# Two rows of x stored early into the output by ScalarE, in a one-core decode layer

## The chip, the cores and the metric

The kernel runs on one core of a Trainium2 chip. The metric is device time in microseconds (us), from one launch; lower is better. Three runs of the kernel before gave 137.84, 137.99 and 138.12 us, median 137.99.

A core has TensorE (PE in the profile; its weight loads are PEld), VectorE (DVE), ScalarE (ACT), GpSimd (POOL) and SyncE (SP). SP and ACT issue transfers; each has a queue of its own, and the packets of both run on the same 16 DMA engines.

## The reference

One decoding step (one token for each of 4 sequences) of a pre-norm layer: attention over the last 2048 cached keys with 32 query heads on 4 key-value heads, then a gated feed-forward. Cut to what is computed:

```
h  = x + A(layernorm(x))
h2 = h + B(layernorm(h))                      # the output, 4 x 1 x 1024, bf16

A(x):  q = x @ wq                             # wq 1024 x 4096
       p = softmax(q k^T * Dh**-0.5)          # k, v: the last 2048 of 8192 rows, 4 batches, 4 kv heads
       return (p v) @ wo                      # wo 4096 x 1024
B(x):  return (silu(x @ w1) * (x @ w3)) @ w2  # w1, w3 1024 x 3584, w2 3584 x 1024
```

All inputs are bf16. Nearly all bytes are weights and cache; x itself is 8 KB.

## The kernel before, in words

The kernel is a single stream of loads with work hung on it. `plan` lists the loads in order: wq (with a narrow "side" load that brings the end of its last rows in 1 KB pieces), the keys, the values, wo, w1, w3 and w2 in four pieces of 17, 7, 3 and 1 rows. `load_next` issues the next entry, always from SP (L94, L102, L120, L126), into a ring of 80K columns in SBUF. A piece is issued as soon as its place in the ring is free, which is when TensorE has read what lay there.

The stages follow the loads: the first norm and q (L178 to L282), the transposes of k and the scores (L312 to L332), softmax (L335 to L361), the values (L379 to L389), wo (L409 to L417), the second norm (L423 to L451), the gate w1 and the up projection w3 (`gate_up`, L454), and the down projection w2 (`down`, L490). The wide tiles hold four column blocks one below the other: partition 32j + 8b of a wide tile holds column block j of sequence b. `x_q` is x in that form, 256 columns for each j and b, the other partitions zero. It is loaded by two DMAs of SP (L169) and read only once, where it is added to the attention's output (L424).

Around the change: the gate's product `g_ps` goes through ScalarE's exponential into `eg` (L471, with a table load before it), VectorE makes `1/(1 + eg)` and multiplies it with the gate (L472 to L475), TensorE does w3, VectorE multiplies and transposes (L478, L481), TensorE does w2. The two halves of the result are copied into `res` by VectorE (L513) and ScalarE (L514), and ScalarE issues the one store of the output (L515): 16 rows of `res`, 512 bytes each. ScalarE computes nothing between L471 and L514.

The tile framework orders the work. Each DMA gets one of eight completion semaphores ("lanes" 0 to 7, `DMAHW0` to `DMAHW7`) in turn. A DMA that takes a lane waits until the lane's previous DMA has landed; a reader waits for the lane of the DMA that it needs. An instruction holds few waits, so further ones stand ahead of it on the same engine as instructions that only wait. At the end of the program (L541) SP goes through all lanes and the engines' semaphores in five waits, two semaphores each, in this order: lanes 3 and 2, lanes 4 and 1, lanes 5 and 0, lane 6 and VectorE, lane 7 and ScalarE. Then the engines meet at two barriers and the program ends. In the kernel before, the four pieces of w2 have lanes 3, 4, 5 and 6, and the output's store has lane 7.

Of the kernel before, what the change touches and what calls it, by code (L numbers as in the profile page):

```python
# [11 lines left out]
ACT = mybir.ActivationFunctionType  # L12
# [7 lines left out]
def kernel(  # L20
# [13 lines left out]
    nc = tc.nc  # L34
# [15 lines left out]
    out_flat = out.flatten_outer_dims()  # L50
# [16 lines left out]
    RS = QD // B  # L67
    CQ = Hq * Dh // JG
    CG = D // JG
    CF = F // JG  # L70
    HF = CF // 2
# [94 lines left out]
    x_q = act.tile([P, CG], BF16)  # L166
    nc.vector.memset(x_q[:], 0.0)
    for c in range(2):
        nc.sync.dma_start(  # L169
            out=x_q[c * 2 * QD : (c + 1) * 2 * QD : RS, :],  # L170
            in_=x_flat.rearrange("b (j c) -> j b c", j=JG)[2 * c : 2 * c + 2],
# [7 lines left out]
    for c in range(2):  # L179
# [8 lines left out]
        out=xn[:], in0=x_sb[:], scalar1=mv[:, 0:1], scalar2=rstd[:, 0:1],  # L188
# [14 lines left out]
    for r0, ne, ns in SETS:  # L203
# [3 lines left out]
            out=xs[:, len(sl) : len(sl) + ns, : ne * 4].rearrange("b l (i s) -> b l i s", s=4),  # L207
            in_=v[:, KC - 1, :, :, :],
        )
        for l in range(ns):  # L210
            nc.tensor.transpose(
                out=ts_ps[: ne * 4, len(sl), :], in_=xs[:, len(sl), : ne * 4], identity=ident[:B, :B]
# [4 lines left out]
    for _, ne, ns in SETS:  # L217
# [14 lines left out]
        out=perm[:].rearrange("p (h dq) -> p h dq", dq=JG),  # L232
        in_=ident[:].rearrange("p (dq h) -> p h dq", dq=JG),
# [12 lines left out]
    for j in range(2, JG):  # L246
        nc.vector.tensor_tensor(
            out=same[:, 0, :], in0=same[:, 0, :], in1=ident[:, j * QD : (j + 1) * QD], op=ALU.add
# [35 lines left out]
    for r in range(REP):  # L284
        nc.tensor.transpose(out=qt_ps[:, r, :], in_=q_sb[:, r * Dh : (r + 1) * Dh], identity=ident[:])
    nc.vector.tensor_copy(
        out=qz[:, :, : Hkv * QD].rearrange("p b (g z) -> p b g z", g=Hkv)[:, :, :, :REP],
        in_=qt_ps[:].rearrange("p r (g x) -> p x g r", g=Hkv)[:, :B, :, :],
# [24 lines left out]
    for u, (b, n) in enumerate(units):  # L313
        k_v = loaded["k"][b]
        kT = ktpool.tile([P, NJ, P], BF16, tag="kT")
        for t in range(NJ // TB):
            kt_ps = psA.tile([P, TB, P], BF16, tag=f"kt{nt % 4}")
            for jj in range(TB):
                nc.tensor.transpose(  # L319
                    out=kt_ps[:, jj, :], in_=k_v[:, n * NJ + t * TB + jj, :], identity=ident[:]  # L320
# [21 lines left out]
        out=Pm[:], in_=scores_ps[:], func=ACT.Exp, bias=nmax[:], scale=1.0, accum_out=rsum[:]  # L342
# [6 lines left out]
    for c in range(NSB):  # L349
# [4 lines left out]
        for g in range(Hkv):  # L354
            if g % 2 == 0:
                nc.vector.tensor_scalar(  # L356
                    out=z[:, :, g, :], in0=pt_ps[:], scalar1=mask[:, g : g + 1], scalar2=None, op0=ALU.mult
# [10 lines left out]
        out=Dm[:], in0=ident[:].rearrange("p (g b r) -> p b g r", g=Hkv, b=B),  # L368
# [38 lines left out]
    g_ps = psB.tile([P, 2, 512], FP32, tag="g")  # L407
    u_ps = psB.tile([P, 2, 512], FP32, tag="u")
    for i in range(IO):  # L409
# [34 lines left out]
        out=hn[:], in0=h1[:], scalar1=tot[:, 0:1], scalar2=rstd2[:, 0:1],  # L444
# [5 lines left out]
        out=hnT[:].rearrange("p k x -> p (k x)"), in_=hn[:].rearrange("q (c k) -> q k c", k=KC)  # L450
# [3 lines left out]
    def gate_up(kind, out_ps):  # L454
# [13 lines left out]

    gate_up("w1", g_ps)
    eg = wide.tile([P, 2, HF], FP32, tag="w4k")  # L470
    nc.scalar.activation(out=eg[:], in_=g_ps[:, :, :HF], func=ACT.Exp, scale=-1.0)  # L471
    nc.vector.tensor_scalar_add(out=eg[:], in0=eg[:], scalar1=1.0)  # L472
    nc.vector.reciprocal(out=eg[:], in_=eg[:])  # L473
    gs = wide.tile([P, 2, HF], FP32, tag="w4k")
# [7 lines left out]
        out=hgT[:].rearrange("p i x -> p (i x)"),  # L482
        in_=hg[:].rearrange("q s c -> q (s c)").rearrange("q (c i) -> q i c", i=IF),
# [62 lines left out]
```

## Time and profile before

| what | value |
|---|---|
| three runs, median (lowest to highest) | 137.99 us (137.84 to 138.12) |
| span of the profiled execution | 136.0 us |
| HBM read | 55.59 MB, 409 GB/s over the span |
| packets of SP's queue (q1), share of 16 engines | 95.6% |
| packets of ScalarE's queue (q10) | 36, 0.02 MB |
| busy: PE, PEld, DVE, ACT, POOL | 72.3, 46.1, 43.9, 31.0, 1.7 us |

The span runs from the first to the last instruction. The profile gives the profiled execution no time of its own beyond its span; the median of the runs is 1.99 us above it, and that difference is taken as what lies around the span. A share of 95.6% of all 16 DMA engines says that the loads hardly ever pause. Line numbers are those of the kernel before; from L472 on, the same statement stands two lines further down after the change.

### The profile page before, as it was taken

To read this page: it belongs to the slowest core of one execution; us is meant where nothing else is said; L and a number is where in the kernel's file an instruction comes from. 1 tells how busy PE (TensorE), PEld (TensorE's weight loads), DVE (VectorE), ACT (ScalarE), POOL (GpSimd) and SP (SyncE) were. 2 spreads that over 40 slices of the span, in tenths; PEclk is the share of its full clock that TensorE was granted. 3 is DMA by queue.
4 is the path that set the end of the run, shared out by engine and by line. 5 is a ranking of instruction groups with operands and counts; after the bars stand their busy time and mean duration, and the time that the engine had idled before them with its cause. 6 is when DMAs were issued, how large, how long until landed. Compare 5 with 4: busy or idle time off the path is not lost.

```text
span 136.0 us, 2436 instructions
## 1 busy us (share of the span) xinstructions
PE 72.3 (53%) x1096; PEld 46.1 (34%) x1096; DVE 43.9 (32%) x79; ACT 31.0 (23%) x36; POOL 1.7 (1%) x8
## 2 busy tenths in 40 slices
PE   0004920979898989810525916791097000970981
PEld 0002300268374756500014905570043000430870
DVE  5055000043344444470994001206200596026010
ACT  3000000015555555609294300000001400000000
POOL 5000000000000000000000000000000000000000
PEclk9999975557999999985555555568556855568568
DMA  5999999999999999999989999989989899999970
GB/s 155 464 463 406 412 420 414 429 424 439 424 439 424 424 443 426 410 552 453 463 347 463 463 410 405 477 354 494 439 371 494 371 472 401 399 420 407 424 298 5
DMA packets 2650, 55.75 MB, mean 410 GB/s; under 512 B 296, under 2 KB 464, under 8 KB 720
## 3 DMA queue, kind: packets, MB, share of 16 engines
q1 hardware_dynamic: 2604, 55.58, 95.6%
q8 instruction: 8, 0.13, 0.3%
q10 hardware_dynamic: 36, 0.02, 0.0%
q14 instruction: 2, 0.02, 0.0%
HBM read 55.59 MB, written 0.01 MB: 409 GB/s over the span
## 4 chain that ended last, share of the span: by engine, by line
DMA 54%; PE 25%; ACT 11%; DVE 5%; SPq 2%; issue 1%; ACTq 0%
DMA ring<-in_B_w_dram 38%; DMA ring<-in_A_wq_dram 15%; PE kt_ps L319 11%; ACT kT L325 5%; PE scores_ps L304 5%; ACT z L360 3%; PE q_ps L263 3%; DVE rmax L336 2%; ACT Pm L341 2%; PE OT_ps L382 2%; DVE pT L350 1%; SPq L120 1%; PE g_ps L459 1%; DVE z L356 1%; ACT L341 1%
## 5 line engine op out<-in xcount | busy, mean ns | idle before, releaser
L325 ACT COPY kT<-kt_ps 128x1024 bf16<-128x1024 bf16 x16 | 15.9, 1013 | 13.4 <-PE kt_ps L319 13.4
L319 PE MATMUL kt_ps<-ident,ring 128*128 128x128 bf16 x256 | 18.0, 232 | 0.0
L319 PEld LDWEIGHTS <-ring 128*128 128x128 bf16 x256 | 16.0, 105 | 4.9 <-issue 4.9
L323 DVE COPY kT<-kt_ps 128x1024 bf16<-128x1024 bf16 x16 | 11.1, 692 | 16.5 <-PE kt_ps L319 16.5
L459 PEld LDWEIGHTS <-hnT 128*32 128x32 bf16 x128 | 5.5, 143 | 21.8 <-issue 19.2
L382 PE MATMUL OT_ps<-z,ring 128*128 128x32 bf16 x256 | 7.5, 188 | 8.5 <-ACT z L360 5.0
L459 PE MATMUL u_ps<-ring,hnT 128*32 128x448 bf16 x64 | 6.0, 563 | 11.0 <-DMA ring<-in_B_w_dram 11.0
L304 PE MATMUL scores_ps<-kT,qz 128*32 128x512 bf16 x64 | 9.9, 609 | 2.9 <-ACT kT L325 2.9
L263 PE MATMUL q_ps<-ring,xnT 128*4 128x512 bf16 x63 | 6.7, 595 | 7.8 <-DMA ring<-in_A_wq_dram 7.8
L382 PEld LDWEIGHTS <-ring 128*128 128x128 bf16 x256 | 7.4, 104 | 9.2 <-issue 9.2
L459 PE MATMUL g_ps<-ring,hnT 128*32 128x448 bf16 x64 | 5.9, 558 | 4.9 <-DMA ring<-in_B_w_dram 4.9
L492 PEld LDWEIGHTS <-hgT 128*32 128x32 bf16 x156 | 4.9, 134 | 6.2 <-issue 5.7
L411 PE MATMUL y_ps<-ring,o 128*32 128x256 bf16 x128 | 5.9, 371 | 0.8 <-DVE o L398 0.8
L514 ACT CAST res<-yb_ps 128x128 bf16<-128x128 f32 x1 | 0.3, 266 | 26.1 <-PE yb_ps L492 26.1
L492 PE MATMUL y_ps<-ring,hgT 128*32 128x256 bf16 x68 | 3.8, 419 | 4.4 <-DMA ring<-in_B_w_dram 4.4
L360 ACT ACTIVATE z<-pt_ps,mask 128x512 bf16<-128x512 f32 x8 | 5.3, 687 | 3.5 <-DVE z L356 3.5
L352 PE MATMUL pt_ps<-pT,perm 128*128 128x512 bf16 x4 | 2.4, 607 | 6.8 <-DVE pT L350 6.8
L263 PEld LDWEIGHTS <-xnT 128*4 128x4 bf16 x63 | 2.0, 115 | 11.7 <-issue 11.6
L194 PE MATMUL tp_ps<-ident,xn 4*128 4x4 bf16 x8 | 0.7, 200 | 10.0 <-DVE xn L187 10.0
L356 DVE TENSOR_SCALAR z<-pt_ps,mask 128x512 bf16<-128x512 f32 x8 | 5.5, 741 | 1.2 <-ACT z L360 0.8
L473 DVE RECIPROCAL eg<-eg 128x896 f32<-128x896 f32 x1 | 5.8, 5753 | 0.0
L411 PEld LDWEIGHTS <-o 128*32 128x32 bf16 x128 | 4.4, 131 | 3.1 <-DVE o L398 1.9
(85 smaller groups left out, 50.1 us busy)
## 6 DMA issues: line engine op xcount, KB each, us to landing
ring<-in_B_w_dram SPq DMA_DIRECT2D x2, 7168.0 KB, 22.5
ring<-in_A_k_cache_dram SPq DMA_DIRECT2D x4, 2048.0 KB, 27.6
ring<-in_A_v_cache_dram SPq DMA_DIRECT2D x4, 2048.0 KB, 29.2
ring<-in_B_w_dram SPq DMA_DIRECT2D x1, 4352.0 KB
ring<-in_A_wq_dram SPq DMA_DIRECT2D x1, 4096.0 KB, 12.2
ring<-in_A_wq_dram SPq DMA_DIRECT2D x1, 3968.0 KB
ring<-in_B_w_dram SPq DMA_DIRECT2D x1, 1792.0 KB
ring<-in_B_w_dram SPq DMA_DIRECT2D x1, 768.0 KB
```

The lines of the kernel that those rows point to most:

```text
L263: nc.tensor.matmul(q_ps[QD * g : QD * g + B, hf * 512 : hf * 512 + n], lhsT=xnT[:, kc, :], rhs=wq_t[:, c0 : c0 + n], start=(kc == 0), stop ...
L304: nc.tensor.matmul(scores_ps[QD * g : QD * (g + 1), n * 512 : (n + 1) * 512], lhsT=qz_v[:, z0 : z0 + QD], rhs=kT_v[:, g, :, :], start=(b = ...
L319: nc.tensor.transpose(out=kt_ps[:, jj, :], in_=k_v[:, n * NJ + t * TB + jj, :], identity=ident[:])
L323: nc.vector.tensor_copy(out=kT[:, t * TB : (t + 1) * TB, :], in_=kt_ps[:])
L325: nc.scalar.copy(out=kT[:, t * TB : (t + 1) * TB, :], in_=kt_ps[:])
L356: nc.vector.tensor_scalar(out=z[:, :, g, :], in0=pt_ps[:], scalar1=mask[:, g : g + 1], scalar2=None, op0=ALU.mult)
L360: nc.scalar.mul(out=z[:, :, g, :], in_=pt_ps[:], mul=mask[:, g : g + 1])
L382: nc.tensor.matmul(OT_ps[:, b, :], lhsT=loaded["v"][b][:, j, :], rhs=PTz[j // NJ][:, (j % NJ) * B + b, :, :], start=(j == 0), stop=(j == J ...
L411: nc.tensor.matmul(y_ps[QD * j : QD * (j + 1), :], lhsT=o4[:, i, :, :].rearrange("p b s -> p (b s)"), rhs=loaded["wo"][i][:, j * CG : (j + ...
L459: nc.tensor.matmul(out_ps[QD * j : QD * (j + 1), hf, :HF], lhsT=hnT[:, k, :], rhs=loaded[kind][k][:, c0 : c0 + HF], start=(k == 0), stop=( ...
L473: nc.vector.reciprocal(out=eg[:], in_=eg[:])
L492: nc.tensor.matmul(out_ps[QD * j : QD * (j + 1), :n], lhsT=hgT[:, i, :], rhs=loaded["w2"][i][:, j * CG + c0 : j * CG + c0 + n], **kw,)
```

## The change

Behind the exponential, ScalarE also issues a store of two rows of `x_q` (partitions 0 and 8: the first 256 columns of x for sequences 0 and 1) into the first 256 columns of the output's rows 0 and 1, 512 bytes each. `tc.issue_after` places it behind the exponential in ScalarE's order. The output's store at the end writes these places again, so that the output is the same.

```diff
     gate_up("w1", g_ps)
     eg = wide.tile([P, 2, HF], FP32, tag="w4k")
-    nc.scalar.activation(out=eg[:], in_=g_ps[:, :, :HF], func=ACT.Exp, scale=-1.0)
+    exp_i = nc.scalar.activation(out=eg[:], in_=g_ps[:, :, :HF], func=ACT.Exp, scale=-1.0)
+    with tc.issue_after(exp_i.ins):
+        nc.scalar.dma_start(out=out_flat[0:2, 0:CG], in_=x_q[0 : 2 * RS : RS, :])
     nc.vector.tensor_scalar_add(out=eg[:], in0=eg[:], scalar1=1.0)
```

In the built program two more things differ. The early store takes lane 3, so every DMA behind it moves on by one lane: the pieces of w2 have lanes 4 to 7, the output's store lane 0. And the output's store, which writes where the early store wrote, waits for lane 3 (the early store) beside its own lane, VectorE and ScalarE:

```
before  L515 DMACopy out_dram<-res 4x4x256 [waits DMAHW7_49,DVE_49,Activation_49]
after   L473 DMACopy out_dram<-x_q 2x256 [waits DMAHW4_49,DMAHW3_49]
after   L517 DMACopy out_dram<-res 4x4x256 [waits DMAHW0_49,DMAHW3_49,DVE_49,Activation_49]
```

The order of all other instructions on every engine is the same, and so is the order of SP's five waits at the end.

## The prediction

> **What bounds the kernel now.** I read the page's queue table first, then the chain that ended last, then the timeline and the transfers of the last microseconds.
>
> ```profile
> span 136.0 us, 2436 instructions
> ...
> q1 hardware_dynamic: 2604, 55.58, 95.6%
> ...
> q10 hardware_dynamic: 36, 0.02, 0.0%
> ...
> DMA 54%; PE 25%; ACT 11%; DVE 5%; SPq 2%; issue 1%; ACTq 0%
> ```
>
> SP's queue q1 keeps the 16 DMA engines busy for 95.6% of the span: the stream of weights is the bound. In the chain, in order of time, the end reads:
>
> ```profile
> 76.27 22.49 DMA ring<-in_B_w_dram
> ...
> 98.80 1.68 PE g_ps L459 x14
> 100.48 29.74 DMA ring<-in_B_w_dram
> ...
> 130.27 0.30 PE ya_ps L492 x3
> ```
>
> From 76 us to 130.2 us the chain is nothing but weights landing, save 1.7 us. So whatever delays the stream delays the end, and whatever lies on ScalarE or VectorE between 100 and 130 us does not, unless it is long. The timeline of that stretch and of the end:
>
> ```profile
> 106.06 0.92 ACT L471 ACTIVATE eg<-g_ps 128x896 f32<-128x896 f32 x1
> ...
> 107.67 5.75 DVE L473 RECIPROCAL eg<-eg 128x896 f32<-128x896 f32 x1
> ...
> 115.70 5.95 PE L459 MATMUL u_ps<-ring,hnT 128*32 128x448 bf16 x64 [11.03 <-DMA ring<-in_B_w_dram]
> ...
> 133.02 0.29 DVE L513 CAST res<-ya_ps 128x128 bf16<-128x128 f32 x1 [2.67 <-PE yb_ps L492]
> 133.08 0.27 ACT L514 CAST res<-yb_ps 128x128 bf16<-128x128 f32 x1 [26.10 <-PE yb_ps L492]
> 133.39 0.64 ACTq L515 DMA_DIRECT2D out_dram<-res  x1
> ```
>
> To be seen here: ScalarE is idle for 26.10 us behind the exponential, and from 133.39 us on only the output's store and the end of the program are left, 2.6 us. The store's own transfers, from the DMA view of 133 to 136 us, and SP's wait for them:
>
> ```profile
> q10 hardware_dynamic: 20, 0.01, 1.1%
> ...
> SPq L541 <- DMA out_dram<-res: 1.8, 1, 1.8
> ...
> L541 SPq EVENT_SEMAPHORE  x7: 17/28/649, 125.9 to 135.9; - x7
> ...
> L515 ACTq EVENT_SEMAPHORE  x1: 266/266/266, 133.1 to 133.1; - x1
> ```
>
> Twenty packets (16 of 512 bytes, 4 that count the semaphore up) take 1.1% of 16 x 3 us, 0.53 us, 26 ns each. SP waits 1.8 us for the store, from its issue at 133.39 to 135.18. The trace's packet records split that: issue 0.639 us, first packet 1.27 us after the issue began (134.660), last packet over at 134.834, last count of the semaphore at 135.164.
>
> **The change, part by part.**
>
> 1. ScalarE's issue of the early store. ScalarE's own issues took 0.563 and 0.265 us (the two loads of x, L158) and 0.639 us (the output's store). Even 0.64 us lies in the 26.10 us of idle time; VectorE waits for the exponential alone, which comes first. The cover would be gone only for a store as long as that idle time. 0 us. The early store's waits, for x_q's load and for its lane's previous DMA (the second load of v, landed by 52.9), are long met, so nothing queues behind it.
>
> 2. Its transfer. Two packets of 512 bytes and two that count the semaphore go between the packets of w3. The packets of the output's store took 27 to 39 ns and the counts 9 ns; those of x's loads, 1 KB beside a full stream at 6.1 to 7.6 us, 46 and 9 ns, and on the engine of the last of them SP's next packet began within 4 ns of each end. So an engine that carries one loses 36 to 55 ns, and the other 14 nothing. Whether the end feels it depends on whether that engine is among the last. The 16 counts of w2's last piece come between 130.94 and 132.68 us, twelve of them in the last 0.44 us, and the engines that carried x's loads and the narrow side load end in that group. Ends: 0 and 0.055 us. I take 0.03, the middle, as one of two such engines may be the last.
>
> The Trainium skill, "DMA: Bandwidth & Descriptors", section "Why a DMA increments its semaphore by 16 and not by 1", says that a DMA of k rows from these queues uses the lowest-numbered k engines. If so the early store sits on two of the four engines of the x loads, and the sum would have 0.055 here rather than 0.03.
>
> 3. SP's waits for the loads of w2. Every piece has a new lane, and one more waiting instruction stands before the piece of 17 rows: a met wait on SP costs about 0.05 us (0.053 from 100.861 to 100.915 us at L94). That load is issued at 91.60 and its first bytes are wanted behind w3's, which land at 115.66: 24 us of cover. The other lanes were free by 52.7 us. 0 us.
>
> 4. ScalarE's waits before the output's store. One more met wait, about 0.05 us, runs beside the cast L514: the existing wait row lasts 266 ns, the length of the cast, because it ends with VectorE's cast at 133.31 and its semaphore. The extra one fits within. 0 us, and 0.05 as the upper end.
>
> 5. SP's waits at the end. Before, the output's store has lane 7, named in the last of five waits, so SP is through as soon as it lands: that wait starts at 135.181 and the next instruction at 135.246, 0.065 us. After, the store has lane 0, named in the third; the fourth (lane 6, VectorE) and fifth (lane 7, ScalarE) come behind it, both met. Two more met waits on the path that ends the program: 2 x 0.053 to 2 x 0.065. I take 0.12 us. Ends 0.11 and 0.13.
>
> 6. What a second use of the store's path may save. No row shows a second store, so it is bounded. Issue: the two loads of x have the same form and took 0.563 and then 0.265 us, a gain of 0.30 if the difference is a first use. Against it: the side loads, also four rows outside, took 0.965 us with 20 pieces in each and 0.801 with 12, 20.5 ns a piece; for the store's 4 pieces this line gives 0.637, and it took 0.639. No first-use cost is left in it. From issue to first packet: 1.27 us for the store, 0.96 for x's first load, itself a first use; the difference, 0.31, less the 0.08 of the longer issue, bounds the gain at 0.23. Together 0 to 0.53 us. I take 0: the side loads are the nearest row in form, and x's first load was no slower for being first. The loss on this side is bounded by 0, since nothing is added to the last store's path but item 4.
>
> 7. What the write does to the stream. A store into HBM in the middle of reads is not in the trace. The output's last packet was over at 134.834 and its count showed at 135.164, 0.33 us, nothing else running. If an engine held SP's packets back until its write is confirmed, it would lose 0.33 us. Against it: the count packets themselves took 9 ns, so the engine was not held in them, and SP's own loads end in such counts without a pause. Ends 0 and 0.33; I take 0, nearest to the x loads amid the stream.
>
> Here a rule of the skill speaks against the change. The same page, section "Queues, rings and completion order", says that the count is a strongly ordered write that lands only after every earlier write of that engine, across its queues; its section "Latency and other measured facts" puts an HBM access at 2 us under high load. If this stopped the engine, the loss would be an estimated 2 us, the time 140.1 us.
>
> Sum against the profiled execution: 136.0 + 0.03 + 0.12 = 136.15 us. The median of the runs is 1.99 us above its span, so 138.14 us, 0.11% above 137.99. Some 0.2%, 0.28 us, is about what a measurement of this kernel can tell from no change: I forecast no change, leaning to slower.
>
> **The rivals.**
>
> - A: the first store of a queue pays a first-use cost, and the early one takes it off the end. For: 0.563 against 0.265 us at L158, 1.27 us to the first packet. Against: item 6's line through the side loads. At its full bound: 137.99 - 0.53 + 0.15 = 137.61 us. It makes the kernel faster from a saving of 0.15 us on, and by over 0.2% from 0.43 us on.
> - B: the write holds the engines that carry it until it is confirmed. Place: two DMA engines at about 107 us, in w3; the loss stays with them to the end of w2, for there is no gap to make it up. For: the stream has no slack, and these engines are in the late group. Against: 9 ns for a count. Price 0.33: 137.99 + 0.33 + 0.055 + 0.12 = 138.5 us. It decides (over 0.2%) from a hold of 0.13 us on, the rest of the sum counted.
> - C: nothing can be seen at all: the two waits overlap the barrier that follows, the packets miss the last engine. 137.99 us. For: other engines are at the barrier already. Against: SP arrives last at it.
>
> **How the numbers follow.** My forecast's own case and C together I give 0.46; both end within 0.2%. B, with a hold anywhere from 0.13 us up, and the chance that items 2, 4 and 5 lie at their upper ends (0.055 + 0.05 + 0.13 = 0.235) with some noise on top, 0.31. A beyond 0.43 us, or a smaller saving with the end waits hidden, 0.23. The range reaches to both: below to A's 137.61 less 0.06, because the end waits may be hidden with it, above to B's 138.5 plus the 0.1 us by which single runs differ: 137.55 to 138.6.
>
> **What would show it.** Item 1: ACTq's issue at about 106 to 107 us, VectorE's L474 unmoved. Item 2: w2's last landing within 0.06 us of 132.68. Item 5: about 0.12 us more between the landing of the output's store and the end of the span. Item 6: the last issue again 0.64 us, its first packet 1.27 us behind it; less is rival A. Item 7: w2's last piece landing 0.1 us later or more is rival B. I would be wrong if the last store's path has a first-use cost that rows of loads cannot show, or if writes and reads disturb each other in a way that loads among themselves do not.

## The result

The changed kernel took 138.23 us (median, 138.01 to 138.48), the kernel before 137.94 us (137.73 to 138.12), 19 runs each; the measured ratio is 1.0025, 95% interval 1.0019 to 1.0032, and that of the medians 1.0021: +0.3 us. A second comparison, made with the experiments, gave 1.0014 (1.0005 to 1.0023). The forecast of 138.14 us lies close by, and its range held the time; but a term that it took as nothing was the larger part of the loss.

### The profile after

The page, and the chain that ended last in order of time:

```profile
span 136.4 us, 2439 instructions
...
q1 hardware_dynamic: 2604, 55.58, 95.3%
...
q10 hardware_dynamic: 40, 0.02, 0.0%
```

```profile
98.94 1.68 PE g_ps L459 x15
100.63 29.67 DMA ring<-in_B_w_dram
...
130.33 0.30 PE ya_ps L494 x4
```

Three instructions and four packets are new (of the packets two are rows and two are counts); the stream of loads stands as it stood, and from 100 to 130 us it takes 29.67 us against 29.74. In the timeline of ScalarE and of the end:

```profile
105.04 1.28 ACT L471 ACT_TABLE_LOAD   x1 [12.87 <-PE g_ps L459]
105.16 0.72 ACTq L473 DMA_DIRECT2D out_dram<-x_q  x1
106.34 0.92 ACT L471 ACTIVATE eg<-g_ps 128x896 f32<-128x896 f32 x1
...
133.28 0.27 ACT L516 CAST res<-yb_ps 128x128 bf16<-128x128 f32 x1 [26.02 <-PE yb_ps L494]
133.75 0.60 ACTq L517 DMA_DIRECT2D out_dram<-res  x1
```

The early store is issued beside the table load and takes none of the exponential's time (0.01 us from table load to exponential, as before). At the end, the cast begins at 133.28 and lasts 0.27, so it is over at 133.54, but the store's issue begins only at 133.75. Before, 133.08 + 0.27 was followed by the issue at 133.39. The waits ahead of that issue (the columns are count, shortest, median and longest ns, first and last start):

```profile
L517 ACTq EVENT_SEMAPHORE  x2: 17/28/38, 133.3 to 133.7; - x2
L517 ACTq DMA_DIRECT2D out_dram<-res x1: 597/597/597, 133.8 to 133.8; - x1
```

The first of the two waits is over at 133.300, the second begins at 133.674. For 0.374 us ScalarE's sequencer, the part of the engine that issues its instructions, did nothing that a row names.

The end, taken apart by the records of the three profiled executions (us; the changed kernel was profiled a second time in the experiments):

| step | before | after | after, second |
|---|---|---|---|
| w2's last landing | 132.680 | 132.758 | 132.664 |
| start of ScalarE's cast | 133.079 | 133.277 | 133.051 |
| end of the cast to the store's issue | 0.044 | 0.208 | 0.226 |
| issue to landing of the store | 1.775 | 1.726 | 1.734 |
| landing to SP's last instruction ahead of the barrier | 0.082 | 0.186 | 0.186 |
| span | 136.00 | 136.42 | 136.22 |

In the second profile the cast starts no later than before, and the span is 0.22 us longer: +0.18 from cast to issue, -0.04 from issue to landing, +0.10 behind the landing, -0.03 ahead of the cast. The first profile has 0.2 us more ahead of the cast, 0.08 of it up to w2's last landing and 0.12 behind that; w1's last landing, at 98.902 against 98.757, was already late ahead of the early store. The second profile shows none of this, and what it was stays open. So two things have to be explained: the sequencer's 0.37 us, and SP's 0.10 us.

### The profile page after: what moved, and what is told of

It reads as the page before. It is cut to its first block, busy times and chain, and to the rows that moved or that the text cites. A ratio compares the mean times of both kernels' runs of the same rounds, so it can differ in the third digit from the quotient of the medians.

```text
span 136.4 us, 2439 instructions
## 1 busy us (share of the span) xinstructions
PE 70.4 (52%) x1096; PEld 44.1 (32%) x1096; DVE 43.9 (32%) x79; ACT 30.9 (23%) x36; POOL 1.7 (1%) x8
## 4 chain that ended last, share of the span: by engine, by line
DMA 55%; PE 22%; ACT 13%; DVE 5%; SPq 2%; issue 1%; ACTq 0%
DMA ring<-in_B_w_dram 40%; DMA ring<-in_A_wq_dram 15%; PE kt_ps L319 9%; ACT kT L325 6%; PE scores_ps L304 5%; ACT z L360 3%; PE q_ps L263 2%; DVE rmax L336 2%; ACT Pm L341 2%; PE OT_ps L382 1%; DVE pT L350 1%; SPq L120 1%; PE g_ps L459 1%; DVE z L356 1%; ACT L341 1%
## 5 line engine op out<-in xcount | busy, mean ns | idle before, releaser
L319 PE MATMUL kt_ps<-ident,ring 128*128 128x128 bf16 x256 | 16.5, 219 | 0.0
L319 PEld LDWEIGHTS <-ring 128*128 128x128 bf16 x256 | 14.4, 98 | 5.0 <-issue 4.9
L382 PEld LDWEIGHTS <-ring 128*128 128x128 bf16 x256 | 7.4, 104 | 9.0 <-issue 9.0
L281 DVE TENSOR_SCALAR q_sb<-q_ps 128x512 bf16<-128x512 f32 x1 | 0.7, 692 | 14.1 <-PE q_ps L263 14.1
```

Of the source, the lines that this page charges most:

```text
L319: nc.tensor.transpose(out=kt_ps[:, jj, :], in_=k_v[:, n * NJ + t * TB + jj, :], identity=ident[:])
L382: nc.tensor.matmul(OT_ps[:, b, :], lhsT=loaded["v"][b][:, j, :], rhs=PTz[j // NJ][:, (j % NJ) * B + b, :, :], start=(j == 0), stop=(j == J ...
```

## The experiments

The theory at this point: the end waits cost SP 0.10 us, and the sequencer's delay belongs to a place in ScalarE's instruction stream. The rivals: the delay comes with the extra wait or the early store's semaphore; the write costs the stream (B); the end waits cost nothing (C). The runs were spread over three chips; every ratio below is to the kernel before, run on the same chip, and the microseconds beside it are its excess over 1 times the median of that kernel, 137.86 to 137.88 us.

### The change again

The changed kernel, nothing edited.

> The changed kernel again, as the yardstick of this chip. Theory T: its loss has two parts at the end of the program. SP needs two more waits behind the landing of the output's store (0.10 us in the two profiles), and ScalarE's sequencer reaches its second wait before that store 0.37 us late, which puts the store's issue 0.21 us behind the end of the cast instead of 0.04 (0.16 us). The first packet comes 0.04 us sooner, so +0.22 to +0.30 us against before. Rival W (the write costs the stream of loads): the same total here, but w2's last piece lands later.

Measured: 1.0014 (1.0005 to 1.0023), +0.19 us; the column "after, second" above. Both parts are there again. The time is a little under the +0.22 to +0.30 us expected, which its interval reaches, and w2's last piece lands as before (132.664 against 132.680), against the rival.

### Six copies behind the early store

```diff
     with tc.issue_after(exp_i.ins):
         nc.scalar.dma_start(out=out_flat[0:2, 0:CG], in_=x_q[0 : 2 * RS : RS, :])
+    idle = act.tile([P, 6], FP32)
+    with tc.issue_after(exp_i.ins):
+        for k in range(6):
+            nc.scalar.copy(out=idle[:, k : k + 1], in_=eps_t[:])
```

> The change, with six one-column copies on ScalarE behind the early store, in its idle time (they write a scratch tile that nobody reads). They move ScalarE's later instructions six places on. Theory T says that the sequencer's delay belongs to a place in ScalarE's instruction stream, not to the wait that stands there: it now falls among the copies at about 107 us, the store's issue comes 0.05 to 0.08 us behind the cast, and the time is 0.12 to 0.16 us below the change, about +0.10 us against before. The rival, that the delay comes with the extra wait or with the early store's semaphore: no difference from the change.

Measured: 1.0035 (1.0022 to 1.0048), +0.48 us, where +0.10 was expected. The delay has left the place before the store, as the theory says: the same two waits stand there, and the issue follows the cast again at once. Its line in the timeline, and its waits:

```profile
133.58 0.27 ACT L520 CAST res<-yb_ps 128x128 bf16<-128x128 f32 x1 [26.06 <-PE yb_ps L498]
133.89 0.59 ACTq L521 DMA_DIRECT2D out_dram<-res  x1
```

```profile
L521 ACTq EVENT_SEMAPHORE  x2: 17/114/211, 133.6 to 133.6; - x2
```

The number of waits is therefore not the cause. No row shows the delay among the copies either: they start every 0.08 to 0.09 us, from 106.879 us on. But everything is 0.5 us late by then, and the transfers of 105 to 116 us show something new (queue, kind, packets, MB, share of 16 engines). It is the line of q14; the one packet of q8 is there in the kernel before too, and the four of q10 are the early store's:

```profile
q8 instruction: 1, 0.02, 0.5%
q14 instruction: 1, 0.01, 0.2%
q10 hardware_dynamic: 4, 0.00, 0.0%
```

An 8 KB instruction packet of queue q14, 309 ns, sits at 111.04 us, among the loads of w3. In the kernel before this packet comes at 135.652, in the changed kernel at 134.327 and 134.135, both times 0.65 to 0.67 us behind the end of the sequencer's delay. From w1's last landing to w3's it is 17.34 us here and 16.89 to 16.91 in the kernel before and both profiles of the changed one. So the stretch with the packet in it is 0.44 us longer.

### Three copies, no early store

```diff
-    nc.scalar.activation(out=eg[:], in_=g_ps[:, :, :HF], func=ACT.Exp, scale=-1.0)
+    exp_i = nc.scalar.activation(out=eg[:], in_=g_ps[:, :, :HF], func=ACT.Exp, scale=-1.0)
+    idle = act.tile([P, 3], FP32)
+    with tc.issue_after(exp_i.ins):
+        for k in range(3):
+            nc.scalar.copy(out=idle[:, k : k + 1], in_=eps_t[:])
```

> The kernel before, no early store, with three such copies on ScalarE, which move its later instructions on by as many places as the change does. Theory T: the wait before the output's store now stands at the place where the changed kernel was late; the store's issue begins 0.15 to 0.2 us behind the end of the cast, +0.10 to +0.16 us against before, and the end waits of SP stay as they were. Rivals (the early store, its semaphore or its write cause the delay): no change, within 0.05 us.

Measured: 1.0033 (1.002 to 1.0045), +0.46 us, and not for the reason expected: the store's issue follows the cast by 0.043 us, and q14's packet is at 108.84 us, in w3's loads; w1 to w3 takes 17.36 us, 0.45 more. TensorE's rows show it: before, the wait for w3 (in brackets) was 11.03 us, and the work on w2 began at 126.06 us.

```profile
116.21 5.63 PE L459 MATMUL u_ps<-ring,hnT 128*32 128x448 bf16 x64 [11.58 <-DMA ring<-in_B_w_dram]
126.58 3.82 PE L496 MATMUL y_ps<-ring,hgT 128*32 128x256 bf16 x68 [4.74 <-DMA ring<-in_B_w_dram]
```

Three instructions that do nothing, in 26 us of idle time, cost more than the early store. Of the theory the first half stands (a place in the stream of instructions, since only ScalarE's program differs), but where the place falls was not yet understood. Counted in the trace's rows of ScalarE that carry a line of the kernel, the gap stands behind the 63rd in all eight profiles that show one. Here the 63rd is the cast itself, which stands waiting for TensorE from 107 us on; that the stop is passed in this waiting time is a reading of q14's packet at 108.84 us, no row shows it. In the changed kernel the 63rd is the first of the two waits.

### Two copies, no early store

As above, with two copies:

```diff
-    idle = act.tile([P, 3], FP32)
+    idle = act.tile([P, 2], FP32)
...
-        for k in range(3):
+        for k in range(2):
```

> The kernel before with two copies on ScalarE, one fewer than the run that moved ScalarE's 8 KB instruction fetch (queue q14) from the end of the program to 109 us, into w3's loads. Theory P: the sequencer works 0.39 us on a fetch where it reaches the end of a block of instructions, and an 8 KB packet follows 0.67 us later; where the place falls directly ahead of the output's store, the store is late, with no early store in the program. By the order of instructions the place should now be the wait or the issue of that store: q14's packet at 134 to 135 us, the issue 0.15 to 0.25 us behind the cast instead of 0.04, +0.10 to +0.20 us against before. If the fetch has already moved into the loads: w3's landing 0.44 us later and +0.45 us. The rival, that the delay needs the early store: neither, and no change.

Measured: 1.0026 (1.0015 to 1.0037), +0.36 us. Now the 63rd instruction is the wait and the 64th is the store's issue:

```profile
133.08 0.27 ACT L518 CAST res<-yb_ps 128x128 bf16<-128x128 f32 x1 [25.64 <-PE yb_ps L496]
133.74 0.64 ACTq L519 DMA_DIRECT2D out_dram<-res  x1
```

```profile
L519 ACTq EVENT_SEMAPHORE  x1: 265/265/265, 133.1 to 133.1; - x1
```

The wait is over at 133.353, the issue begins at 133.741: 0.39 us, with one wait, no early store and the lanes of before. q14's packet follows at 134.383. In the expectation the gap from the cast to the issue was 0.15 to 0.25 us and the loss 0.10 to 0.20; the gap is 0.39, for nothing hides any of it here, while in the changed kernel the delay starts as the cast starts and 0.24 us of it lies beside the cast.

### The change with one wait fewer

```diff
-        nc.scalar.dma_start(out=out_flat[0:2, 0:CG], in_=x_q[0 : 2 * RS : RS, :])
+        nc.scalar.dma_start(out=out_flat[0:2, 0:CG], in_=xn[0:2, 0:CG])
```

> The change, with the early store taken from two rows of the normalised x (512 bytes each) instead of x_q: it needs no wait for a load, so ScalarE has one instruction fewer than in the change. Theory P: that is worse, not better. ScalarE's instructions move back by one, the end of a block falls directly ahead of the issue of the output's store, where nothing hides it: issue 0.39 us behind the cast instead of 0.2, and the two waits of SP behind the landing stay. +0.40 to +0.50 us against before, 0.15 to 0.25 above the change. Rival, that the delay comes with the number of waits on ScalarE or with the store of x_q: the same as the change or a little less.

Measured: 1.0045 (1.0033 to 1.0057), +0.6 us, the slowest of all, with less to do than the change; +0.40 to +0.50 was expected, and the rival, no more than the change, falls. The cast and the issue:

```profile
133.08 0.27 ACT L516 CAST res<-yb_ps 128x128 bf16<-128x128 f32 x1 [27.20 <-PE yb_ps L494]
133.73 0.65 ACTq L517 DMA_DIRECT2D out_dram<-res  x1
```

The issue begins 0.385 us behind the cast, and 0.185 us lie between the landing and SP's last instruction. The rest of the 0.6 is not all explained: in this profile the store's landing comes 0.40 us behind its last packet, and 0.32 to 0.34 in the other profiles of before and after.

### The early store without its side effects

```diff
-    for c in range(2):
-        nc.scalar.dma_start(out=x_sb[:, c * 512 : (c + 1) * 512], in_=x_flat[:, c * 512 : (c + 1) * 512])
+    nc.scalar.dma_start(out=x_sb[:], in_=x_flat)
...
-        nc.scalar.dma_start(out=out_flat[0:2, 0:CG], in_=x_q[0 : 2 * RS : RS, :])
+        nc.scalar.dma_start(out=out_flat[0:2, 0:CG], in_=xn[0:2, 0:CG])
```

> The early store, with both side effects taken out: x_sb is loaded by one DMA of ScalarE instead of two (one instruction and one lane fewer), and the store's source is two rows of the normalised x, 512 bytes each, which need no wait of their own; so ScalarE has one instruction more than before instead of three, and the output's store has lane 7. Theory: the store itself costs nothing in the stream and saves 0.04 us on the last store; q14's packet comes behind the last store, the issue 0.04 us behind the cast, SP's last wait ends with the landing. Time -0.10 to +0.03 us against before, not to be told from it. Rival W (the write costs the stream): +0.1 us or more still, w2's last landing late. If the fetch still falls ahead of the store: +0.12 to +0.18 us.

Measured: 1.0001 (0.9992 to 1.001). The loss is gone with the early store still there:

```profile
133.25 0.27 ACT L515 CAST res<-yb_ps 128x128 bf16<-128x128 f32 x1 [27.53 <-PE yb_ps L493]
133.56 0.64 ACTq L516 DMA_DIRECT2D out_dram<-res  x1
```

The sequencer's delay is still in the program, and now harmless: the store's issue ends at 134.201, and the next instruction of ScalarE begins at 134.586 instead of 0.04 us later, while all wait for the landing. The control, the kernel before with one load of x_sb:

> The control for the run with the early store and one load of x_sb: the kernel before with x_sb loaded by one DMA, no early store. The output's store has lane 6, so SP has one met wait behind its landing, +0.05 us; x arrives earlier, which the start should not show, as wq's loads set it. Theory: -0.05 to +0.08 us against before.

Measured: 1.0015 (1.0004 to 1.0027), +0.21 us (by the medians, 138.23 against 137.88, +0.35), more than expected. One met wait of SP, that is a wait already fulfilled when SP comes to it, is there (landing to its last instruction 0.143 us instead of 0.082), and with one instruction fewer on ScalarE the place moves into the barriers at the end. ScalarE's rows there, first of this run, then of the kernel before:

```profile
L540 ACTq EVENT_SEMAPHORE  x2: 17/17/17, 135.5 to 136.2; - x2
L540 ACTq DRAIN  x1: 128/128/128, 135.9 to 135.9; - x1
```

```profile
L541 ACTq EVENT_SEMAPHORE  x2: 17/17/17, 135.5 to 135.9; - x2
L541 ACTq DRAIN  x1: 8/8/8, 135.6 to 135.6; - x1
```

From the start of the first barrier wait to that of the DRAIN it is 0.42 us here, 0.09 before, and the second barrier waits for it. So the run with the early store and one load of x_sb is 0.14% faster than its own control without the store. The early store brings one instruction and one lane: the one puts the place where nothing waits for it, the other takes away SP's met wait. That it equals the kernel before is what the theory said; that it beats its control is accounted for by these two, and no row shows a gain by the store itself.

### The end waits alone

The kernel before with x_q's load in three DMAs (every later lane moves on by one), and with four 64-byte loads behind w2 (by four):

```diff
-    for c in range(2):
+    for a, e in ((0, 2), (2, 3), (3, 4)):
         nc.sync.dma_start(
-            out=x_q[c * 2 * QD : (c + 1) * 2 * QD : RS, :],
-            in_=x_flat.rearrange("b (j c) -> j b c", j=JG)[2 * c : 2 * c + 2],
+            out=x_q[a * QD : e * QD : RS, :],
+            in_=x_flat.rearrange("b (j c) -> j b c", j=JG)[a:e],
         )
```

```diff
+    spare = act.tile([B, 32], BF16)
...
                 load_next(3)
+                for r in range(4):
+                    nc.sync.dma_start(out=spare[r : r + 1, :], in_=x_flat[r : r + 1, 0:32])
```

> The kernel before, no early store, but the load of x_q in three DMAs in place of two, so that every later DMA moves one lane on and the output's store has lane 0, as in the change; ScalarE's instructions are the same as before. Theory T: SP has two met waits behind the landing of the store, 0.10 us more between that landing and the end, +0.10 us in all (0.05 to 0.15). Rival C of the prediction (the two waits are hidden in the barrier): no change.

> The kernel before, no early store, with four loads of 64 bytes into a scratch tile issued by SP behind the last piece of w2, so that the output's store has lane 3, named in the first of SP's five waits; ScalarE's instructions are those of before. Theory: four met waits behind the landing of the store instead of none, 0.06 us each: landing to the end's first barrier 0.29 us instead of 0.08, +0.20 to +0.28 us against before. Rival C, that these waits cost nothing because something else ends later: no change beyond 0.05 us.

Measured: 1.0007 (0.9998 to 1.0016) for the first, +0.10 us, which by the time alone is not told from nothing; in its profile 0.186 us lie between the landing and SP's last instruction, as in the changed kernel. For the second 1.0021 (1.0012 to 1.0031), +0.29 us. SP's waits at the end there, and in the kernel before:

```profile
L545 SPq EVENT_SEMAPHORE  x7: 17/28/28, 135.4 to 136.5; - x7
```

```profile
L541 SPq EVENT_SEMAPHORE  x3: 17/17/28, 135.2 to 135.9; - x3
```

Seven waits against three behind 135 us, four more, and 0.339 us from landing to SP's last instruction against 0.082: 0.064 us for each met wait. This profile's stream was already 0.36 us late at w1's last landing (99.119 against 98.757), so that its span is not longer by the waits alone. But from SP's last instruction ahead of the barrier to the end of the span it is 0.75 us in both: what the waits take is paid in full. Rival C falls.

### The change with its lane put back

```diff
-    for c in range(2):
-        nc.sync.dma_start(
-            out=x_q[c * 2 * QD : (c + 1) * 2 * QD : RS, :],
-            in_=x_flat.rearrange("b (j c) -> j b c", j=JG)[2 * c : 2 * c + 2],
-        )
+    nc.sync.dma_start(out=x_q[0:P:RS, :], in_=x_flat.rearrange("b (j c) -> j b c", j=JG))
```

> The change, with x_q's load as one DMA instead of two: every later DMA moves one lane back and the output's store has lane 7 again, named in SP's last wait; ScalarE's instructions are those of the change. Theory: the two waits behind the landing go (0.19 us from landing to the end's first barrier become 0.08), the sequencer's delay before the store stays (issue 0.2 us behind the cast); +0.10 to +0.18 us against before, 0.10 below the change. Rival C: same as the change.

Measured: 1.0018 (1.0009 to 1.0027), +0.25 us, which is not below the change, where 0.10 us below it was expected. The waits went as expected (0.082 us behind the landing), the delay stayed (issue 0.209 us behind the cast), but the landing itself came 0.53 us behind the last packet, against 0.32 to 0.34, and took the 0.2 us back. (The profiled execution, 138.33 us, was one of four at 138.28 to 138.37; the other seven took 137.98 to 138.14, and what their landing did is not known.) The run of two copies has 0.49 us there, that with one wait fewer 0.40. All three have q14's packet near the store's packets (134.38 to 134.47), but so have the two profiles of the changed kernel, with 0.32 and 0.34. What sets this last step was not found. One thing the five profiles do show: q14's packet ends 0.20 and 0.16 us before the store's first packet in the two of the changed kernel, and 0.11, 0.09 and 0.08 us before it in those with 0.40, 0.49 and 0.53. The closer it comes, the later the landing; that is an order of five numbers and was not tested.

### Eight times the store

The run without side effects, its early store made 8 KB:

```diff
-        nc.scalar.dma_start(out=out_flat[0:2, 0:CG], in_=xn[0:2, 0:CG])
+        nc.scalar.dma_start(out=out_flat, in_=xn[:])
```

> The run with the early store and neither side effect, its early store made eight times as large: all four rows of the normalised x, 2 KB each, over four DMA engines (8 KB). Theory: the write is nothing but its packets, about 0.09 us on each of four engines; 0 to 0.1 us over the run with the small store, -0.05 to +0.12 us against before. Rival W, that a write in the midst of the loads holds its engine until it is confirmed (0.33 us or more): w3's and w2's last landings 0.2 us later or more, +0.2 us at least.

Measured: 1.0006 (0.9998 to 1.0015). Four packets of 2 KB took 84 ns each at 108.6 to 109.0 us and their counts 9 ns; w1 to w3 takes 16.89 us, w2's last landing is at 132.733. Here a write in the midst of the loads cost its packets at most. Rival B falls, also at eight times the size.

## Why the prediction was right, and where not

| term of the prediction | predicted, us | measured, us |
|---|---|---|
| 1 issue of the early store | 0 | 0 (0.72 us of issue beside the table load) |
| 2 its transfer | 0.03 (0 to 0.055) | none seen; w1's landing to w3's 16.89 and 16.90 against 16.91 |
| 3 SP's waits for w2's loads | 0 | 0 |
| 4 ScalarE's waits before the store | 0 (up to 0.05) | 0.16 and 0.18 |
| 5 SP's waits at the end | 0.12 (0.11 to 0.13) | 0.10 |
| 6 a second use of the store's path | 0 (gain up to 0.53) | gain 0.05 and 0.04 |
| 7 the write in the stream | 0 (up to 0.33) | 0, also with 8 KB |
| sum | 0.15 | 0.22 by the second profile; 0.19 and 0.3 by the times |

Item 4 failed. I priced the extra wait as an instruction, 0.05 us beside the cast, and asked only what it waits for. What it does, with the two new instructions ahead of it, is move the program behind it. The step that I took as nothing, three more instructions on an idle engine, was the larger part of the loss, and its upper end of 0.05 us was too low: no row of the profile before shows the delay, because there the 63rd row is the DRAIN behind the store's issue, over at 134.552 us, and ScalarE then waits for the others until 135.467 anyway. q14's packet at 135.652 us was the only sign of it. That the cause is the place and not the store is shown from both sides: two copies without any store make the same delay, and the store with the place put right and its lane kept makes no loss. That the stop belongs to the fetch of the next block of instructions is inferred: a packet of kind "instruction" follows it each time, but it begins 0.64 to 0.93 us after the stop is over, so that the sequencer did not wait for the packet itself.

Item 5 was right in mechanism and 0.02 us too large for two waits. Item 6: the gain is there in the profiles of the changed kernel, almost all in the issue, 0.60 instead of 0.64 us; the runs whose early store reads adjacent rows of the normalised x have 0.64, so it goes with the strided source; why was not tested, and it is too small to matter. Rival A falls: 0.04 us is not the 0.15 from which it decides. Rivals B and C fall by the runs above.

The time came out a little above the forecast: in one comparison just above the 0.2% named as the bound (its interval reaches down to 0.19%), in the other within it. "No change, leaning to slower" was the right side; the reason given for the lean was less than half of it. That the range held the time is in part luck: its upper part was drawn for rival B, and what filled it was item 4 at over three times its upper end.

The Trainium skill, "Runtime: NRT & Kernel Launch", section "Instruction fetch mechanics", says that an engine fetches its next block of instructions while it runs the current one and that crossing a boundary is mostly hidden. Here the stop of ScalarE's sequencer, if it is such a crossing, was 0.37 to 0.41 us long in the eight profiles that show it; it cost time ahead of the last store and in the end barrier, and none where the engine was waiting for the store's landing. Where the packet fell into the saturated stream of loads, the stream came 0.44 us later.

No run beat the kernel before. The best that the early store reached here was to cost nothing.

## What to carry to other kernels

An added instruction is not free because its engine is idle: it moves every later instruction of that engine against the fixed place where the sequencer stops and an instruction packet follows. Look where the instruction packets of the profile fall, and try to keep that place from standing directly ahead of the last store and the packet out of a full stream of loads. An added DMA also shifts the completion lanes of all later ones; the last store is best waited for last, as each met wait behind it cost 0.06 us here.

## What the runs showed of the hardware

- ScalarE's sequencer stood still for 0.37 to 0.41 us behind the 63rd of its rows, and an 8 KB packet on queue q14 followed. With one instruction fewer than the kernel before, the delay lay in the end barrier (+0.21 us); with one more, behind the store's issue (0); with two more, directly ahead of it (+0.36 us); with the change's three more, between its two waits. In every run another packet of this kind lies amid the loads at 58 to 61 us; what that one costs was not tested.
- Where that packet, there 309 ns long, fell into w3's loads, the stream came 0.44 us later (17.34 and 17.36 us against 16.89 to 16.94 in all other profiles for the same stretch). Why this is more than its own length was not tested.
- A store of two 512-byte rows by ScalarE, issued amid SP's loads, had its packets 3.2 to 5.1 us after its issue ended and its counts 2.1 us later still; neither it nor an 8 KB store delayed the loads by an amount that the runs could show.
- A store from two rows eight partitions apart took 0.72 us to issue, one from two adjacent rows 0.26 us.
